# Two products of batch 1 move from VectorE to TensorE, by transposed blocks, in a fused decode-layer gradient kernel

## The chip, the core and the metric

The kernel runs on one core of a Trainium2 chip. The metric is the time of one execution on the device in microseconds; every time below is one of the core's own or comes from the hardware profile of one execution. The engines are named as in the profile: PE is TensorE's matrix products, PEld its weight loads, DVE is VectorE, ACT is ScalarE, POOL is GpSimd, SP is the engine that issues most loads.

## What is computed

The reference is one decoder layer for one new token per sequence, two sequences (batch 0 and batch 1), with its output and the gradients of seven of its inputs:

```python
h  = x + attention(layernorm(x), k_cache, v_cache, wq) @ wo   # 32 heads of 128, 4096 cached keys
h2 = h + relu(layernorm(h) @ w1) @ w2                         # 640 -> 1728 -> 640
out, vjp = jax.vjp(f, x, k_cache, v_cache, wq, wo, w1, w2)
return out, *vjp(grad_out)
```

x has 640 numbers per sequence. The caches and their gradients are the bulk: K and V hold 64 pairs of (batch, head) of 4096 x 128 bf16, one MB each, and so do their gradients. Two steps of the backward pass matter here, once per batch:

- the gradient at the input of the MLP, `w1 x gradient`: for each of the 640 rows of w1, the sum over 1728 columns of w1 times the gradient of the hidden layer (`ghfc`);
- the gradient at the attention's output, `wo x gh1`: for each of the 32 x 128 rows of wo, the sum over 640 columns of wo times `gh1`, the gradient of h.

Both sums run along the free dimension of the weights as they lie in memory (a row of the weight on a partition), which is why they are awkward for TensorE: it sums over partitions.

## The kernel before

**Two phases over 64 pairs.** The first phase (`p1_iter`, index i) reads K and V of a pair, makes the scores, the softmax and the attention output. The second (`p2_iter`, index j) reads V again (called W), makes the gradient of the probabilities by transposing W in blocks (`pair_transpose`, L436, copied out of PSUM by ScalarE at L441, multiplied at L449), and then writes two MB per pair: `gV` and `gK`, each made by VectorE in two halves (L822) and stored by GpSimd's queue (L879 and L860). An order written out by hand (`plan`) interleaves the two phases: from i = 41 on, one turn j for every two i, and after the last i the turns j alone. The second phase takes the pairs in the order of `turns`; batch 1 begins at j = 32 with its last five heads.

**A middle per batch.** `middle_gen(b)` stands between the phases of a batch: output projection, layer norm, the hidden layer (L748), for batch 1 the same again for both batches in another order (L759), then `ghfc`, then the product with w1, a layer norm backward (`ln_bwd`, whose column sum is a small product, L222), giving `gh1c`, then the products with wo. Each wo group (up to eight heads, `go_group`) yields `goc`, `gom` and `negdot`, which the turns of those heads need.

For both products the gradient is spread over all partitions (`bcast_cols`, into `fbc` and `hbc`), and VectorE multiplies and sums along the free dimension in one instruction (`ttr`, L649): 15 of 576 columns for w1 and 32 of 640 for wo, for each batch.

**Background queues.** The middle, the outer products of the weights' gradients (`fin_gen`, which makes tiles `ot` in `outer_rows`, L926, L935, L933, L937) and the gradient at x (`gx_gen`) are Python generators. Each step of a turn lets each of three queues go on by a credit: the middle by 0.8 a step up to turn 32 and 0.45 later, `fin_gen` by 0.65, `gx_gen` by 0.45. A generator says with `yield 0.9` what a piece costs. A `ttr` also waits for a slot (`turn()`): three slots a turn up to turn 32, two later. `wait(n)` lets 2n steps go by in this part. `fin_gen` begins once the w1 product is through (`("w1", 1)`), `gx_gen` goes to work once all of batch 1's wo products are.

**PSUM.** There are eight banks. 0 and 1 take the transposes, 2 and 3 the rows of a turn, 7 the middle's small results. Once the first phase is over and w1 is done, the outer products of `fin_gen` rotate over banks 4, 5 and 6; while `gx_gen` sums in bank 6, over 4 and 5:

```python
banks.update(sps=[2, 3], o=[4, 5, 6])   # when fin_gen starts
banks["o"].remove(6)                    # when gx_gen starts
```

`gx_gen` already has the form that the change gives to the two products: eight blocks of wq are transposed by TensorE (L993), copied from PSUM by ScalarE (L995), and multiplied with a column one group later (L1003).

Of the kernel before, what the change touches and what calls it, by code (L numbers as in the profile page):

```python
# [7 lines left out]
FP32 = mybir.dt.float32  # L8
# [7 lines left out]
def kernel(  # L16
# [41 lines left out]
    def f_kc(c):  # L58
        return 128 if c < NFF else F_rem
# [600 lines left out]
    def one(src, b):  # L660
        return src[:, :, b]

    def go_group(b, h0, h1, hbc):

        hs = slice(h0, h1)
        n = h1 - h0
        go32 = small.tile([128, GH], FP32, tag="go32", bufs=1, name="go32")
        for k in range(n):
            yield from turn()
            ttr(wo_t[:, h0 + k, :], hbc[:], go32[:, k:k + 1], D)  # L670
            yield 0.9
        nc.vector.tensor_copy(out=goc[:, hs, b], in_=go32[:, 0:n])
        pr = small.tile([128, GH], FP32, tag="pr", bufs=1, name="pr")
        nc.vector.tensor_tensor(out=pr[:, 0:n], in0=goc[:, hs, b], in1=OU[:, b, hs], op=ALU.mult)
        yield from wait(2)
        pair_rows(gom, goc, hs, slice(b, b + 1))
        yield from wait(2)
        d_ps = pst([128, 2, GH], FP32, "mid", "d_ps")
        nc.tensor.matmul(d_ps[:, 0, 0:n], lhsT=ones_f32, rhs=pr[:, 0:n], start=True, stop=True)
        for k in range(n):  # L680
            h = h0 + k
            nc.tensor.matmul(d_ps[:, 1, k:k + 1], lhsT=MTs.pop((b, h))[:], rhs=goc[:, h, b:b + 1],
                             start=True, stop=True)
        nc.vector.tensor_scalar(out=negdot[:, hs, b], in0=d_ps[:, 0, 0:n], scalar1=-1.0, scalar2=None, op0=ALU.mult)
        ud = small.tile([128, GH], FP32, tag="ud", bufs=1, name="ud")
        nc.vector.tensor_tensor(out=ud[:, 0:n], in0=Uc[:, b, hs], in1=negdot[:, hs, b], op=ALU.mult)
        mg = small.tile([128, GH], FP32, tag="mg", bufs=1, name="mg")
        nc.vector.tensor_tensor(out=mg[:, 0:n], in0=d_ps[:, 1, 0:n], in1=rt[:, b, hs], op=ALU.mult)
        nc.vector.tensor_tensor(out=ud[:, 0:n], in0=mg[:, 0:n], in1=ud[:, 0:n], op=ALU.add)
        nc.vector.tensor_scalar(out=GQc[:, hs, b], in0=ud[:, 0:n], scalar1=SCALE, scalar2=None, op0=ALU.mult)  # L690
        for h in range(h0, h1):
            done.add(("go", b, h))
        yield

    def mlp_out():

        ml32 = small.tile([128, ND, B], FP32, tag="ml32", bufs=1, name="ml32")
        nc.vector.memset(ml32[:], 0.0)
        for k in range(NW2):
            while free["q"] < 1:  # L700
                yield
            t = load_w2(k, "q", "(p c) d -> p c d")
            yield from wait(12)
            c1 = min(NF, (k + 1) * FP)
            m_ps = pst([128, ND, B], FP32, "mid", "mlp_ps")
            for c in range(ND):
                for cf in range(k * FP, c1):
                    kc = f_kc(cf)
                    nc.tensor.matmul(m_ps[:, c, :], lhsT=t[0:kc, cf - k * FP, c * 128:(c + 1) * 128],
                                     rhs=arow[0:kc, cf, :], start=(cf == k * FP), stop=(cf == c1 - 1))  # L710
            give(t)
            yield
            nc.vector.tensor_tensor(out=ml32[:], in0=m_ps[:], in1=ml32[:], op=ALU.add)
        ml_bf = small.tile([128, ND, B], BF16, tag="ml_bf", bufs=1, name="ml_bf")
        nc.vector.tensor_copy(out=ml_bf[:], in_=ml32[:])
        y_bf = small.tile([128, B, ND], BF16, tag="y_bf", bufs=1, name="y_bf")
        nc.vector.tensor_tensor(out=y_bf[:].rearrange("p b c -> p c b"), in0=h1c[:], in1=ml_bf[:], op=ALU.add)
        yield from wait(3)
        for b in range(B):
            store_row(y_bf[:, b, :], ND, out_0[b].rearrange("s (c p) -> (s c) p", p=128))  # L720
            yield

    def middle_gen(b):
        if o_next[0] < (b + 1) * H // OG:
# [41 lines left out]
        nc.vector.tensor_single_scalar(out=mask[:], in_=acol[:, :, b], scalar=0.0, op=ALU.is_gt)  # L766
        nc.vector.tensor_tensor(out=ghfc[:, :, b], in0=ga[:, b, :], in1=mask[:], op=ALU.mult)
        yield from wait(3)
        fbc = cols.tile([128, Dff], BF16, tag="fbc", name="fbc")
        gx2 = small.tile([128, 1, ND], FP32, tag="gx2", bufs=1, name="gx2")  # L770
        gx2p = small.tile([128, ND, 3], FP32, tag="gx2p", bufs=1, name="gx2p")
        FW = Dff // 3
        spread_f = bcast_cols(one(ghfc, b), NF, f_kc, fbc)
        have = 0
        for k in range(3):
            while have < min(Dff, (k + 1) * FW):
                next(spread_f)
                have += 512
                yield
            for c in range(ND):  # L780
                yield from turn()
                ttr(w1_t[:, c, k * FW:(k + 1) * FW], fbc[:, k * FW:(k + 1) * FW], gx2p[:, c, k:k + 1], FW)
                yield 0.85
        nc.vector.reduce_sum(out=gx2[:, 0, :], in_=gx2p[:], axis=AX.X)
        yield ("w1", b)
        yield from ln_bwd(gx2[:], x2c[:, :, b:b + 1], rstd2[:, b:b + 1], gc[:, :, b:b + 1], gh1c[:, :, b:b + 1], 1)
        hbc = cols.tile([128, D], BF16, tag="rowbc", name="hbc")
        yield from bcast_cols(one(gh1c, b), ND, lambda c: 128, hbc)
        yield ("gh1", b)

        first = H - KEPT[b]
        bounds = [(first, first + 2), (first + 2, H)] if b == 0 else [(first, H)]
        bounds += [(h, min(first, h + GH)) for h in range(0, first, GH)]
        for h0, h1 in bounds:
            yield from go_group(b, h0, h1, hbc)
        if b > 0:
            yield from mlp_out()

# [166 lines left out]
    def gx_gen(fin):  # L965
        tiles = []

        def fetch():
            while len(tiles) < ND and free["q"] > 0:
                t = take("q", [128, HD], "wqs")  # L970
                nc.sync.dma_start(out=t[:], in_=wq_r[:, len(tiles), :])
                tiles.append((t, step[0]))

        while not all(("go", B - 1, h) in done for h in range(H)):
            yield 0.0
        acc = None
        for c in range(ND):
            while c >= len(tiles) or (step[0] < tiles[c][1] + 16 and not forced[0]):
                fetch()
                yield 0.0  # L980
            if acc is None:
                banks["o"].remove(6)
                acc = ps.tile([128, ND, B], FP32, tag="bank6", bufs=1, name="gx_ps")
            t = tiles[c][0]
            todo = list(range(H))
            prev = None
            for t0 in range(0, len(todo) + GT, GT):
                part = todo[t0:t0 + GT]
                nxt = None
                if part:  # L990
                    t_ps = pst([128, GT, 128], BF16, "tps", "t_ps")
                    for x, h in enumerate(part):
                        nc.tensor.transpose(t_ps[:, x, :], t[:, h * 128:(h + 1) * 128], ident_bf[:])  # L993
                    t_sb = mats.tile([128, GT, 128], BF16, tag="XT", bufs=5, name="t_sb")
                    nc.scalar.copy(out=t_sb[:, 0:len(part), :], in_=t_ps[:, 0:len(part), :])  # L995
                    nxt = (t_sb, part)
                    if t0 + GT >= len(todo):
                        give(t)
                        fetch()
                    yield 0.9  # L1000
                if prev is not None:
                    for x, h in enumerate(prev[1]):
                        nc.tensor.matmul(acc[:, c, :], lhsT=prev[0][:, x, :], rhs=GQc[:, h, :],  # L1003
                                         start=(c == 0 and h == 0), stop=(c == ND - 1 and h == H - 1))
                    yield
                prev = nxt
        gx_bf = fin.tile([128, ND, B], BF16, tag="gxb", name="gx_bf")
        gx1b = fin.tile([128, B, ND], FP32, tag="gx1b", name="gx1b")
        nc.vector.tensor_copy(out=gx1b[:].rearrange("p b c -> p c b"), in_=acc[:])
        banks["o"].append(6)  # L1010
        yield from ln_bwd(gx1b[:], x1c[:], rstd1[:], gh1c[:], gx_bf[:], B)
        for b in range(B):
            gxo = small.tile([128, ND], BF16, tag="gxo", bufs=2, name="gxo")
            nc.vector.tensor_copy(out=gxo[:], in_=gx_bf[:, :, b])
            yield from wait(2)
            store_row(gxo[:], ND, out_1[b].rearrange("s (c p) -> (s c) p", p=128))
            yield
# [107 lines left out]
    for n, (i, j) in enumerate(plan):  # L1125
# [15 lines left out]
        if i is None and ("w1", 1) in done and fin is None:  # L1141
# [1 line left out]
            fin = tc.alloc_tile_pool(name="fin", bufs=1)  # L1143
            big2 = tc.alloc_tile_pool(name="big2", bufs=1)
            more_home("f", big2)
            banks.update(sps=[2, 3], o=[4, 5, 6])
            bg2.append(("fin", fin_gen(fin)))
            bg3.append(("gx", gx_gen(fin)))
        late[0] = all(("go", B - 1, h) in done for h in range(H))
# [84 lines left out]
```

## Time and profile before

| | |
|---|---|
| time, median of 3 | 942.42 us (935.63 to 942.82) |
| profiled execution | 939.0 us, 26775 instructions |
| TensorE products, busy | 766.9 us (82%), 11482 |
| VectorE, busy | 661.9 us (70%), 1237 |
| ScalarE, busy | 551.0 us (59%), 1162 |
| GpSimd, busy | 141.0 us (15%), 249 |
| moved by DMA | 363.02 MB, mean 387 GB/s |

Busy times are sums over the whole span. For TensorE they include the modelled end of each product, so that a busy TensorE is not TensorE at its peak. The clock that is shown with it is a share of its full speed. The busy share of DMA says how long the 16 DMA engines had a packet under way; what they moved in that time stands beside it in GB/s, and the two are not the same.

The stations of batch 1, from the trace: the hidden layer is multiplied again at 511.7 to 519.0 us (L759), the 15 products with w1 run until 562.5 us, the 32 with wo from 574.9 to 704.4 us. The first `ot` is filled at 583.2 us, the last stored at 911.0; `gx_gen` transposes from 731.5 to 868.1 us. The last gK is handed to its queue at 930.4 us.

### The profile page before, as it was taken

How to read it: one execution, taken by the hardware profiler on the slowest of the kernel's cores; microseconds unless marked ns; L12 is line 12 of the kernel's file. 1: busy time of each engine (PE TensorE's matmuls, PEld its weight loads, DVE VectorE, ACT ScalarE, POOL GpSimd, SP SyncE). 2: the span in 40 equal slices, each digit the busy share in tenths (PEclk: the TensorE clock that was granted, in tenths of full speed). 3: DMA queues.
4: the chain of work that ended last, by engine and by line, in shares of the span. 5: the costliest groups of instructions: out<-in, count | busy, mean ns of one | idle time of the engine just before them, and what ended most of it. 6: DMA issues, size and time to landing. Idle time of an engine off the chain costs nothing.

```text
span 939.0 us, 26775 instructions
## 1 busy us (share of the span) xinstructions
PE 766.9 (82%) x11482; PEld 641.4 (68%) x11482; DVE 661.9 (70%) x1237; ACT 551.0 (59%) x1162; POOL 141.0 (15%) x249
## 2 busy tenths in 40 slices
PE   6999898999998888988867838676988877887883
PEld 5878787888787777877757727564766665665652
DVE  4555677766876877786768889787797455465675
ACT  4666565667775776776633626444665564565652
POOL 1222111121001101010012112111121111021111
PEclk9999999999998999998886856556555575575556
DMA  8999999997878999999989999999999999999998
GB/s 348 418 399 410 406 394 410 412 418 266 308 280 341 360 389 423 425 422 414 419 328 369 405 426 395 395 391 376 397 406 398 425 425 423 354 389 377 333 423 364
DMA packets 59478, 363.02 MB, mean 387 GB/s; under 512 B 5696, under 2 KB 15552, under 8 KB 19168
## 3 DMA queue, kind: packets, MB, share of 16 engines
q1 hardware_dynamic: 37920, 212.18, 57.6%
q0 software_dynamic: 18432, 134.23, 34.7%
q10 hardware_dynamic: 3008, 14.91, 4.0%
q8 instruction: 90, 1.47, 0.6%
q14 instruction: 28, 0.23, 0.1%
HBM read 212.16 MB, written 149.13 MB: 385 GB/s over the span
## 4 chain that ended last, share of the span: by engine, by line
PE 39%; DMA 29%; DVE 15%; ACT 10%; issue 5%; POOL 0%; SPq 0%; POOLq 0%; DVEq 0%; ACTq 0%
DMA Kt<-in_A_k_cache_dram 12%; DMA out_dram<-gV 10%; PE t_ps L436 9%; PE m_ps L470 7%; PE t_ps L415 6%; ACT t_sb L420 5%; DMA out_dram<-gK 5%; DVE gV L822 5%; PE s_ps L426 4%; PE o_ps L926 3%; DVE gK L822 3%; DVE pk L477 2%; PE u_ps L495 2%; ACT t_sb L441 2%; DVE junk L649 2%
## 5 line engine op out<-in xcount | busy, mean ns | idle before, releaser
L420 ACT COPY t_sb<-t_ps 128x1024 bf16<-128x1024 bf16 x223 | 216.7, 1012 | 46.6 <-PE t_ps L415 41.8
L441 ACT COPY t_sb<-t_ps 128x512 f32<-128x512 f32 x256 | 149.9, 588 | 159.3 <-PE t_ps L436 156.4
L436 PE MATMUL t_ps<-ident_f,Wt 128*128 128x128 f32 x848 | 195.5, 378 | 3.7 <-ACT t_sb L995 1.4
L470 PE MATMUL m_ps<-pk,Vt 128*128 128x129 bf16 x2048 | 193.3, 224 | 1.0 <-DVE pk L477 0.6
L477 DVE TENSOR_TENSOR pk<-Kt,ep 128x2048 bf16<-128x2048 bf16 x128 | 156.3, 1221 | 34.6 <-ACT ep L520 34.5
L822 DVE TENSOR_TENSOR gK<-rb,gsp 128x2048 bf16<-128x2048 bf16 x128 | 152.2, 1224 | 32.2 <-DMA out_dram<-gK 20.1
L415 PE MATMUL t_ps<-ident_bf,Kt 128*128 128x128 bf16 x2048 | 156.8, 229 | 16.7 <-DMA Kt<-in_A_k_cache_dram 16.6
L822 DVE TENSOR_TENSOR gV<-rb,pp 128x2048 bf16<-128x2048 bf16 x128 | 152.7, 1218 | 23.3 <-DMA out_dram<-gV 20.2
L436 PEld LDWEIGHTS t_ps<-ident_f,Wt 128*128 128x128 f32 x848 | 135.8, 196 | 34.2 <-issue 23.5
L470 PEld LDWEIGHTS <-Vt 128*128 128x128 bf16 x2048 | 130.0, 100 | 29.1 <-issue 29.1
L415 PEld LDWEIGHTS <-Kt 128*128 128x128 bf16 x2048 | 129.3, 102 | 19.1 <-DMA Kt<-in_A_k_cache_dram 18.7
L449 PEld LDWEIGHTS <-t_sb 128*128 128x128 bf16 x2048 | 95.8, 106 | 40.1 <-ACT t_sb L441 18.5
L426 PE MATMUL s_ps<-qc,t_sb 128*128 128x1 bf16 x2048 | 89.2, 164 | 18.1 <-ACT t_sb L420 16.6
L449 PE MATMUL dp_ps<-gom,t_sb 128*128 128x2 bf16 x2048 | 95.2, 167 | 8.9 <-ACT t_sb L441 7.8
L426 PEld LDWEIGHTS <-t_sb 128*128 128x128 bf16 x2048 | 76.0, 97 | 30.6 <-ACT t_sb L420 27.4
L879 POOL DMA_DIRECT2D out_dram<-gV x64 | 34.2, 534 | 288.9 <-DVE gV L822 228.6
L860 POOL DMA_DIRECT2D out_dram<-gK x64 | 34.0, 531 | 279.8 <-DVE gK L822 224.7
L566 POOL COPY P_bf<-ep 128x32 bf16<-128x32 bf16 x40 | 42.6, 1065 | 220.1 <-ACT ep L520 220.1
L935 ACT CAST ot<-o_ps 128x512 bf16<-128x512 f32 (+4 forms) x134 | 60.2, 478 | 23.1 <-DMA out_dram<-ot 11.9
L561 DVE TENSOR_REDUCE rmax<-s_ps 128x1 bf16<-128x32 f32 x64 | 12.3, 193 | 61.4 <-PE s_ps L426 61.3
L649 DVE CUSTOM_DVE_ANT_0 junk<-wo_t,hbc 128x640 bf16<-128x640 bf16 x64 | 52.3, 817 | 0.2
L582 ACT CAST MT<-m_ps 128x128 bf16<-128x128 f32 x64 | 17.1, 267 | 59.1 <-PE m_ps L470 59.1
(194 smaller groups left out, 812.7 us busy)
## 6 DMA issues: line engine op xcount, KB each, us to landing
Kt<-in_A_k_cache_dram SPq DMA_DIRECT2D x64, 1024.0 KB, 14.2
Vt<-in_A_v_cache_dram SPq DMA_DIRECT2D x64, 1024.0 KB, 11.5
out_dram<-gV POOLq DMA_DIRECT2D x64, 1024.0 KB, 10.9
out_dram<-gK POOLq DMA_DIRECT2D x64, 1024.0 KB, 10.3
Wt<-in_A_v_cache_dram SPq DMA_DIRECT2D x53, 1024.0 KB, 10.8
wo_t<-in_A_wo_dram SPq DMA_DIRECT2D x4, 1280.0 KB, 14.1
wqs<-in_A_wq_dram SPq DMA_DIRECT2D x5, 1024.0 KB
wq_t<-in_A_wq_dram SPq DMA_DIRECT2D x5, 960.0 KB, 16.1
```

Source lines behind the costliest of these rows:

```text
L415: nc.tensor.transpose(t_ps[:, j, :], nat[:, g * GT + j, :], ident_bf[:])
L420: nc.scalar.copy(out=t_sb[:], in_=t_ps[:])
L426: nc.tensor.matmul(dst[:, sc:sc + 1], lhsT=t_sb[:, j, :], rhs=vec, start=True, stop=True)
L436: nc.tensor.transpose(t_ps[:, j, :], natf[:, 2 * cc:2 * cc + 2, :].rearrange("p c k -> p (c k)"), ident_f[:])
L441: nc.scalar.copy(out=t_sb[:], in_=t_ps[:])
L449: nc.tensor.matmul(dst[:, sc:sc + 2], lhsT=v[:, j, :, par], rhs=vecs[:, par, :], start=(par == 0), stop=(par == 1))
L470: nc.tensor.matmul(r["m"][:, 0:129], lhsT=r["V"][:, sc, :], rhs=r["pk"][sc // HALF][:, sc % HALF, 0:129], start=(sc == 0), stop=(sc == NSC ...
L477: nc.vector.tensor_tensor(out=p["pk"][k][:, :, 0:128].rearrange("p s (a two) -> p s a two", two=2), in0=p["K"][:, sl, :].rearrange("p s (a ...
L566: (nc.gpsimd if i < P2_AT else nc.vector).tensor_copy(out=P_bf[:, bhp, :], in_=ep[:, :, 0])
L649: nc.vector.tensor_tensor_reduce(out=junk[0:kc, 0:width], in0=in0, in1=in1, scale=1.0, scalar=0.0, op0=ALU.mult, op1=ALU.add, accum_out=acc)
L822: nc.vector.tensor_tensor(out=pairs_view(dst[:, sl, :]), in0=row.rearrange("p (a two) -> p a two", two=2)[:, None, :, :].to_broadcast([128 ...
L935: nc.scalar.copy(out=ot[0:P, k, n0:n0 + nn], in_=o_ps[0:P, 0:nn])
```

## The change

For batch 1 alone, both products leave VectorE. A helper `turned` takes them as groups of up to eight blocks of 128 x 128: TensorE transposes the blocks of a group into a bank of PSUM, ScalarE copies them to `t_sb`, and one turn of the generator later TensorE multiplies them with the gradient's column, summing in bank 6. w1 has 5 x 14 blocks (the last of each 14 has 64 columns) in ten groups, wo has 32 heads of 5 blocks, a group each. The two broadcasts of batch 1 are gone, and the pieces no longer wait for VectorE's slots. Their costs are 0.8 per w1 group and 1.2 per head. What follows the wo product (`go_done`) is as before, but reads the bank. Because bank 6 now holds these sums, the outer products of `fin_gen` have banks 4 and 5 only, until `gx_gen` has given bank 6 back. The purpose is to take the load off VectorE, and to use TensorE for it.

```diff
+    def turned(groups, cost):
+        prev = None
+        for parts in (*groups, None):
+            if prev is not None:
+                for x, (_, kc, dst, vec, first, last) in enumerate(prev[1]):
+                    nc.tensor.matmul(dst, lhsT=prev[0][0:kc, x, :], rhs=vec, start=first, stop=last)
+            if parts is not None:
+                t_ps = pst([128, GT, 128], BF16, "tps", "t_ps")
+                for x, (src, kc, *_) in enumerate(parts):
+                    nc.tensor.transpose(t_ps[0:kc, x, :], src, ident_bf[:])
+                t_sb = mats.tile([128, GT, 128], BF16, tag="XT", bufs=5, name="t_sb")
+                whole = sum(kc == 128 for _, kc, *_ in parts)
+                nc.scalar.copy(out=t_sb[:, 0:whole, :], in_=t_ps[:, 0:whole, :])
...
+            yield cost
+
+    def go_turned(b, h0, h1):
+        acc = ps.tile([128, GH], FP32, tag="bank6", bufs=1, name="go_ps")
+        yield from turned([[(wo_t[:, h, c * 128:(c + 1) * 128], 128, acc[:, h - h0:h - h0 + 1],
+                             gh1c[:, c, b:b + 1], c == 0, c == ND - 1) for c in range(ND)]
+                           for h in range(h0, h1)], 1.2)
+        yield from go_done(b, h0, h1, acc)
+
+    def gx2_turned(b, gx2):
+        acc = ps.tile([128, ND], FP32, tag="bank6", bufs=1, name="gx2_ps")
+        yield from turned([[(w1_t[:, c, cf * 128:cf * 128 + f_kc(cf)], f_kc(cf), acc[:, c:c + 1],
+                             ghfc[0:f_kc(cf), cf, b:b + 1], cf == 0, cf == NF - 1)
+                            for cf in range(f0, min(NF, f0 + GT))]
+                           for c in range(ND) for f0 in range(0, NF, GT)], 0.8)
+        nc.vector.tensor_copy(out=gx2, in_=acc[:])
...
+        if b == B - 1:
+            yield from gx2_turned(b, gx2[:, 0, :])
+        else:
+            yield from gx2_rows(b, gx2)
...
-        hbc = cols.tile([128, D], BF16, tag="rowbc", name="hbc")
-        yield from bcast_cols(one(gh1c, b), ND, lambda c: 128, hbc)
+        if b < B - 1:
+            hbc = cols.tile([128, D], BF16, tag="rowbc", name="hbc")
+            yield from bcast_cols(one(gh1c, b), ND, lambda c: 128, hbc)
...
-            yield from go_group(b, h0, h1, hbc)
+            yield from (go_group(b, h0, h1, hbc) if b < B - 1 else go_turned(b, h0, h1))
...
-                banks["o"].remove(6)
...
-            banks.update(sps=[2, 3], o=[4, 5, 6])
+            banks.update(sps=[2, 3], o=[4, 5])
```

`gx2_rows` holds the lines that stood in `middle_gen` for the w1 product, unchanged, for batch 0.

More of the change, by code (lines that the diff above doesn't have):

```diff
@@ L663, in go_group @@
     def go_group(b, h0, h1, hbc):
-        hs = slice(h0, h1)
-        n = h1 - h0
         go32 = small.tile([128, GH], FP32, tag="go32", bufs=1, name="go32")
-        for k in range(n):
+        for k in range(h1 - h0):
             yield from turn()
@@ L671, in go_group, with go_done @@
             yield 0.9
+        yield from go_done(b, h0, h1, go32)
+    def go_done(b, h0, h1, go32):
+        hs = slice(h0, h1)
+        n = h1 - h0
         nc.vector.tensor_copy(out=goc[:, hs, b], in_=go32[:, 0:n])
@@ L693, in go_group @@
         yield
+    def turned(groups, cost):
[11 more added lines that the diff above has]
+                nc.scalar.copy(out=t_sb[:, 0:whole, :], in_=t_ps[:, 0:whole, :])
+                for x, (_, kc, *_) in enumerate(parts):
+                    if kc < 128:
+                        nc.scalar.copy(out=t_sb[0:kc, x, :], in_=t_ps[0:kc, x, :])
+                prev = (t_sb, parts)
+            yield cost
[12 more added lines that the diff above has]
+        nc.vector.tensor_copy(out=gx2, in_=acc[:])
     def mlp_out():
@@ L721, in mlp_out, with gx2_rows @@
             yield
+    def gx2_rows(b, gx2):
+        fbc = cols.tile([128, Dff], BF16, tag="fbc", name="fbc")
+        gx2p = small.tile([128, ND, 3], FP32, tag="gx2p", bufs=1, name="gx2p")
+        FW = Dff // 3
+        spread_f = bcast_cols(one(ghfc, b), NF, f_kc, fbc)
+        have = 0
+        for k in range(3):
+            while have < min(Dff, (k + 1) * FW):
+                next(spread_f)
+                have += 512
+                yield
+            for c in range(ND):
+                yield from turn()
+                ttr(w1_t[:, c, k * FW:(k + 1) * FW], fbc[:, k * FW:(k + 1) * FW], gx2p[:, c, k:k + 1], FW)
+                yield 0.85
+        nc.vector.reduce_sum(out=gx2[:, 0, :], in_=gx2p[:], axis=AX.X)
     def middle_gen(b):
@@ L768, in middle_gen @@
         yield from wait(3)
-        fbc = cols.tile([128, Dff], BF16, tag="fbc", name="fbc")
         gx2 = small.tile([128, 1, ND], FP32, tag="gx2", bufs=1, name="gx2")
[L771 to L784, printed above, removed]
+        if b == B - 1:
+            yield from gx2_turned(b, gx2[:, 0, :])
+        else:
+            yield from gx2_rows(b, gx2)
         yield ("w1", b)
         yield from ln_bwd(gx2[:], x2c[:, :, b:b + 1], rstd2[:, b:b + 1], gc[:, :, b:b + 1], gh1c[:, :, b:b + 1], 1)
-        hbc = cols.tile([128, D], BF16, tag="rowbc", name="hbc")
-        yield from bcast_cols(one(gh1c, b), ND, lambda c: 128, hbc)
+        if b < B - 1:
+            hbc = cols.tile([128, D], BF16, tag="rowbc", name="hbc")
+            yield from bcast_cols(one(gh1c, b), ND, lambda c: 128, hbc)
         yield ("gh1", b)
```

## The prediction, made before the changed kernel was built

> **What bounds the kernel now.** I read the 40 slices first. In the second half the clock row of TensorE falls to 5 and 6, while the DMA row stays at 9:
>
> ```profile
> PE   6999898999998888988867838676988877887883
> DVE  4555677766876877786768889787797455465675
> ...
> PEclk9999999999998999998886856556555575575556
> DMA  8999999997878999999989999999999999999998
> ```
>
> The change lies where batch 1's products stand, from 525 us (broadcast of `ghfc`) to about 705 us (last L649). Busy time by stretch (PE, weight loads, DVE, ACT, POOL, clock, DMA share, GB/s):
>
> ```profile
> 525.00:566.00 41.00, 21.61 (x286) 17.85 (x283) 35.44 (x59) 16.37 (x31) 6.46 (x15) 0.72 1.01 415
> 566.00:702.00 136.00, 104.41 (x979) 83.16 (x979) 114.53 (x199) 74.47 (x165) 24.68 (x52) 0.56 0.99 393
> 723.00:800.00 77.00, 61.90 (x613) 45.22 (x612) 41.85 (x51) 41.70 (x88) 9.91 (x23) 0.57 1.01 425
> 800.00:880.00 80.00, 64.90 (x631) 49.65 (x630) 42.31 (x57) 47.18 (x90) 10.10 (x21) 0.56 0.94 361
> ```
>
> From 525 to 702 us VectorE is busy 150 of 177 us, and the waits of the same stretch explain nearly all the rest:
>
> ```profile
> DVE gK L822 <- DMA out_dram<-gK: 15.2, 10, 4.0
> PE csum L222 <- DVE lb_mm L290: 13.0, 1, 13.0
> ...
> PE o_ps L926 <- ACT ot L935: 13.0, 6, 5.8
> ACT ot L935 <- DMA out_dram<-ot: 11.9, 2, 6.4
> ...
> PE pr_ps L336 <- DVE goc L672: 8.8, 3, 4.0
> DVE gV L822 <- DMA out_dram<-gV: 8.1, 8, 2.5
> ```
>
> VectorE plus its 23.3 us of waiting for stores to leave a gK or gV buffer fill the stretch: VectorE and DMA share the bound. The DMA engines are always occupied, but at 398 GB/s on average against 425 later, so there is 7% in them. TensorE is busy 126 us (21.61 + 104.41) and idle 51. Its idle time is waiting for others: 13 us at the column sum L222, 9 at `pr_ps`, 13 behind ACT copies into `ot`, 12 of them a store that ACT waited for. That is the room into which the change puts work, and the whole question is whether it is enough.
>
> The later rows are what this stage may turn into. From 723 us `gx_gen` does what the change does, transposing blocks of wq, copying by ACT and multiplying one group behind, with banks 4 and 5 alone for `o_ps`. There VectorE waits 26.4 us for `dp_ps` in 157 us, TensorE paces the turns, and DMA falls to 361 GB/s in the second half.
>
> [...]L993 takes 311 ns (median), and 740 to 765 us, full of transposes, stands at clock 0.50 although TensorE is 60 to 100% busy. [...]the clock falls from 0.84 in 540 to 545 us to 0.50 as the stall of 550 to 564 us begins, and is still 0.50 fifteen microseconds after it. [...]the best 5 us stretch here shows 431[...].
>
> **VectorE, removed.** 15 products of w1 at 0.752 us = 11.3 us, 32 of wo at 0.818 us = 26.2 us: 37.5 us. `go_done`'s small operations stay. VectorE falls from 150 to about 113 us and is no bound any more.
>
> **TensorE, added.** w1: 5 x 14 blocks = 70, wo: 32 x 5 = 160; 230 transposes and 230 one-column products. L993 does 8 transposes in 1.03 us and 16 in 1.89, about 0.125 us each: 28.8 us. Products with one or two columns (L1003, L449) load 8 sets of weights in 0.29 us at best and 0.52 at worst; the middle, 0.045, gives 10.4 us. Less about 2 us of broadcasts: **+37 us**. [...]
>
> **ScalarE, added.** A copy of 1024 elements takes 1.012 us, of 512 0.588, so 640 about 0.69. w1: 5 x 1.01 + 5 x 0.69 + 5 x 0.27 for the 64-row block = 9.9 us; wo: 32 x 0.69 = 22.2 us. Less 3 us of broadcast copies: **+29 us**, 91 to 120 of 177. Not a bound by its sum, but in each group TensorE and ScalarE have to take turns.
>
> **The bank.** `o_ps` has three banks before and two after (bank 6 holds the accumulator). In `outer_rows` product x then waits for copy x-2, which stands just ahead of it, behind the copy of the last turned group on ScalarE. Behind the waiting product stand the next turn's transposes of W, and behind those `gsp`, gK and the store. Lower bound: as now with three banks, 1.8 us without the store's share for 56 products (0.03 each), so nothing. Upper bound: as from 723 to 880 us, 26.6 us for 78 products, 0.34 each: 56 x 0.31 = 17 us. I take 11, since `outer_rows` rests between tiles.
>
> **Order in time.** A turn j of the second phase has 7 background steps, each with 0.8 credit up to turn 32. Before, w1 has 3 slots a turn, 5 turns for 15 products; after, 10 groups and an empty one at 0.8 need 11 steps, 1.6 turns. A group of 8 wo products took 2.7 turns and 1.3 of waits; now 9 x 1.2 / 0.8 = 13.5 steps and 10 of waits, 3.4 turns. So `fin_gen` starts 3 to 4 turns earlier (before: 568 us) and `gx_gen` about 4 (before: 731 us). This alone gains little, as the kernel ends with turns, not with these: the last `ot` store is issued at 911 us, the last gK at 930. Four turns move from this stage's 8.0 us to the end's bare 6.4 us (7 turns from 883 to 928 us): **-6 us**.
>
> **The sum.** TensorE in the stage: 126 + 37 = 163 us; waits that stay: 12 for the store behind `ot`, 4 of the 9 at `pr_ps`, 4 at `rw_ps`, 3 of the 13 at L222, as VectorE is no longer behind; 11 for the bank: 197 us where it had 177. +20 - 6 = +14, with the earlier start of the w2 loads worth about 1: **955 us**. TensorE takes VectorE's place as the bound, because it works at half clock and is stopped by ScalarE in every group.
>
> **Rivals.** (1) *TensorE has room.* With no 13 us stall at L222 the clock stays up: TensorE's sum falls by some 15% (four transposes and their eight products of a turn take 1.15 us per group at half clock, 1.0 at full[...]), to about 139 + 25 = 164 us, under DMA. The stage then goes at DMA's 425 GB/s: 41 us x 415 + 136 x 393 = 70.5 MB, 166 us in place of 177, -11, and no more at the end: **931 us**. For it: 525 to 540 and 585 to 590 us run at clock 1.00 with just the turns' work. Against it: the `gx` stage, the same mix, stays at 0.50. (2) *A draw*: TensorE's waits absorb the added work and DMA keeps its rate of now, whatever VectorE does: **941 us**. For it: DMA share is 0.99 to 1.01 in the stage. (3) *The full price*: TensorE at half clock, the bank at 17 us, the waits at `pr_ps` and L222 stay whole: 163 + 12 + 9 + 4 + 13 + 17 = 218, +41 less 6: 977 us; I count its nearer half with the forecast.
>
> **How the numbers follow.** Forecast with its expensive tail 0.42, room and DMA gain 0.35, draw 0.23. The range goes from a little below the second (its late stage may also gain, 926) to 973, leaving out the rest of the full price. A gain of over 1% needs below 933 us, so it is nearly the room case alone.
>
> **What would show it.** Right: from 525 to 690 us the clock near 0.5 to 0.6, DMA below 390 GB/s, VectorE waiting for `dp_ps` in place of DMA, `o_ps` waiting for ACT by over 10 us more, turns at over 8.5 us; the last wo product some 30 us earlier in turns, less so in time. Wrong: clock above 0.75 there, or `o_ps` not waiting, or the turns at under 8 us with DMA near 420 GB/s; then it is the first rival. That L222 still waits 13 us would say that VectorE was behind for another reason than its products.

## The result

The changed kernel takes 972.94 us (median of 4 runs, 967.87 to 978.38) against 940.43 us for the kernel before, run beside it: ratio 1.0353, 95% interval 1.028 to 1.0426. It is slower by 32 us, where 13 were forecast. The profile below is of the execution of 978.38 us, the slowest of the four.

The 40 slices of the changed kernel, the rows that were shown of the kernel before:

```profile
PE   6999889999988888887877787777887787898982
DVE  4556667866967877778675573455676546465856
PEclk9999999999999989899855665575556555575565
DMA  9999999997788999999799696798899999999998
```

The DMA row has lost its nines just where batch 1's products stand, and VectorE's row has fallen there from digits of 7 to 9 to digits of 3 to 7 (slices 22 to 30). TensorE's row is hardly higher than it was. An engine was relieved, none became full, and the transfers ran dry. The same stretches as before (PE, weight loads, DVE, ACT, POOL, clock, DMA share, GB/s):

```profile
525.00:566.00 41.00, 32.07 (x394) 27.37 (x393) 23.04 (x32) 24.11 (x43) 6.18 (x12) 0.62 0.76 289
566.00:702.00 136.00, 105.08 (x1055) 83.14 (x1053) 70.51 (x120) 74.86 (x156) 17.23 (x39) 0.56 0.85 330
723.00:800.00 77.00, 60.87 (x572) 47.01 (x570) 46.88 (x53) 40.32 (x89) 11.91 (x27) 0.54 1.00 400
800.00:880.00 80.00, 68.56 (x725) 54.70 (x726) 46.36 (x57) 49.08 (x100) 10.68 (x25) 0.59 0.99 392
```

From 525 to 702 us DMA moved 415 and 393 GB/s before, 289 and 330 now. As the work shifts in time, the turns j are the better ruler: the time between the stores of gV, which each turn issues once. Turn 17 begins at 525 us before and at 529 us now.

| turns | before, us | after, us |
|---|---|---|
| 17 to 20 (w1 product of the changed kernel) | 24.1 | 34.1 |
| 17 to 23 | 47.8 | 56.9 |
| 23 to 36 (most of the wo products) | 109.7 | 136.2 |
| 36 to 63 (the rest, with `gx_gen`) | 245.4 | 242.9 |

The loss is 9 us at w1 and 27 at wo, and the later turns give 2.5 back. Turns 17 to 20 and 17 to 36 in the same view, first the kernel before:

```profile
524.93:545.60 20.67, 16.81 (x246) 13.71 (x244) 18.69 (x31) 13.74 (x27) 3.92 (x9) 0.95 1.01 403
524.93:682.40 157.47, 110.18 (x1124) 89.36 (x1122) 130.80 (x224) 79.39 (x172) 26.24 (x57) 0.61 1.00 397
```

and the changed kernel:

```profile
529.34:563.10 33.76, 26.40 (x326) 22.55 (x327) 16.32 (x26) 19.28 (x36) 4.40 (x9) 0.63 0.71 260
529.34:722.48 193.14, 150.45 (x1548) 120.27 (x1549) 104.41 (x163) 106.33 (x214) 26.47 (x57) 0.57 0.84 325
```

(The first line of the kernel before ends 3.4 us short of turn 20, that of the changed kernel 0.4 us.) TensorE is busy 40 us more and idle 43 us of 193, where it was idle 47 of 157: it took the new work but lost hardly any of its waiting. Who waits for whom in these turns of the changed kernel (total in us, times, longest):

```profile
DVE gsp L884 <- PE dp_ps L449: 64.0, 15, 12.0
...
ACT t_sb L712 <- PE t_ps L709: 30.5, 32, 1.5
PE o_ps L975 <- ACT ot L984: 21.3, 23, 1.3
...
PE gx_ps L705 <- ACT t_sb L712: 6.3, 6, 1.2
```

VectorE hardly waits for stores any more (6.4 us in these turns, where it waited 23); it waits for `dp_ps`, that is for TensorE, up to 12 us at a time. TensorE waits for ScalarE, 23 times for an `ot` copy, and ScalarE waits for TensorE, 32 times. What this looks like within a burst of wo heads is in order of time:

```profile
592.58 0.69 PE L709 MATMUL t_ps<-ident_bf,wo_t 128*128 128x128 bf16 x5
...
593.37 0.69 ACT L712 COPY t_sb<-t_ps 128x640 bf16<-128x640 bf16 x1 [1.19 <-PE t_ps L709]
593.96 0.58 ACT L984 CAST ot<-o_ps 96x512 bf16<-96x512 f32 x1
594.59 0.58 PE L975 MATMUL o_ps<-gr,ar 2*96 2x512 bf16 x1 [1.32 <-ACT ot L984]
595.11 0.30 PE L705 MATMUL go_ps<-gh1c,t_sb 128*128 128x1 bf16 x5
...
595.26 0.69 PE L709 MATMUL t_ps<-ident_bf,wo_t 128*128 128x128 bf16 x5
```

One head takes 2.68 us from transposes to transposes, of which TensorE waits 1.32. ScalarE copies the head's blocks, then the older `ot`; only then is one of the two banks free for `o_ps`, and behind `o_ps` on TensorE stands everything else, the next head and the next turn's transposes of W. At w1, where no `o_ps` exists yet, the products themselves wait for the copy of the group just before them (`gx_ps` in the list above).

### The profile page after: what moved, and what is told of

It is laid out like the page before. It is cut to its first block, busy times and chain, and to the rows that moved or that the text cites. A ratio compares the mean times of both kernels' runs of the same rounds, so it can differ in the third digit from the quotient of the medians.

```text
span 976.6 us, 27642 instructions
## 1 busy us (share of the span) xinstructions
PE 807.2 (83%) x11923; PEld 676.2 (69%) x11923; DVE 629.9 (64%) x1146; ACT 576.1 (59%) x1200; POOL 141.6 (14%) x249
## 4 chain that ended last, share of the span: by engine, by line
PE 45%; DMA 23%; ACT 13%; DVE 12%; issue 5%; POOL 0%; ACTq 0%; SPq 0%; POOLq 0%; DVEq 0%
DMA Kt<-in_A_k_cache_dram 15%; PE t_ps L436 13%; PE m_ps L470 6%; PE t_ps L415 5%; PE o_ps L975 5%; DMA out_dram<-gV 4%; ACT t_sb L420 4%; DMA out_dram<-gK 4%; DVE gV L871 3%; PE s_ps L426 3%; ACT t_sb L441 3%; DVE pk L477 3%; PE dp_ps L449 3%; ACT ot L984 2%; PE t_ps L709 2%
## 5 line engine op out<-in xcount | busy, mean ns | idle before, releaser
L436 PE MATMUL t_ps<-ident_f,Wt 128*128 128x128 f32 x848 | 200.9, 387 | 4.4 <-ACT t_sb L420 1.8
L436 PEld LDWEIGHTS t_ps<-ident_f,Wt 128*128 128x128 f32 x848 | 139.2, 200 | 38.4 <-issue 24.5
L871 DVE TENSOR_TENSOR gK<-rb,gsp 128x2048 bf16<-128x2048 bf16 x128 | 152.3, 1224 | 19.9 <-DMA out_dram<-gV 9.9
L884 DVE SCALAR_TENSOR_TENSOR gsp<-dp_ps,negdot,P_bf 128x64 bf16<-128x64 f32 x64 | 18.0, 281 | 93.2 <-PE dp_ps L449 92.1
L561 DVE TENSOR_REDUCE rmax<-s_ps 128x1 bf16<-128x32 f32 x64 | 12.3, 192 | 62.6 <-PE s_ps L426 62.6
## 6 DMA issues: line engine op xcount, KB each, us to landing
Vt<-in_A_v_cache_dram SPq DMA_DIRECT2D x64, 1024.0 KB, 13.1
out_dram<-gV POOLq DMA_DIRECT2D x64, 1024.0 KB, 10.2
```

The lines of the kernel that those rows point to most:

```text
L436: nc.tensor.transpose(t_ps[:, j, :], natf[:, 2 * cc:2 * cc + 2, :].rearrange("p c k -> p (c k)"), ident_f[:])
L871: nc.vector.tensor_tensor(out=pairs_view(dst[:, sl, :]), in0=row.rearrange("p (a two) -> p a two", two=2)[:, None, :, :].to_broadcast([128 ...
```

## The experiments

Each kernel was run beside the kernel before. Three theories stood at the start. *Chain*: TensorE and ScalarE stop each other in each group. *Load*: TensorE's added work at half clock (0.57 in turns 17 to 36 of the changed kernel) does not fit. *Bunching*: too many groups fall into one turn, and DMA runs dry. The first is a sharper form of the forecast's waits, the second is the body of its sum. Below, "turns 17 to 20" are turns j of the second phase; "one turn behind" and "two turns behind" count steps of the generator in `turned`.

| kernel | median us | ratio to before (95%) | turns 17 to 23 | 23 to 36 | 36 to 63 |
|---|---|---|---|---|---|
| changed kernel | 972.94 | 1.0353 (1.028 to 1.0426) | 56.9 | 136.2 | 242.9 |
| w1 alone (x_w1_only) | 944.29 | 1.0046 (1.002 to 1.0071) | 59.5 | 108.5 | 239.7 |
| wo alone (x_wo_only) | 961.11 | 1.0225 (1.0182 to 1.0268) | 49.2 | 121.2 | 254.4 |
| wo product left out (x_no_wo) | 954.15 | 1.0138 (1.0075 to 1.02) | 58.3 | 118.0 | 246.1 |
| copies left out (x_no_copy) | 945.34 | 1.006 (1.0033 to 1.0087) | 48.8 | 119.9 | 245.4 |
| kernel before, two banks (x_two_banks) | 946.26 | 1.0074 (1.0047 to 1.0101) | 47.7 | 107.0 | 251.5 |
| three banks (x_three_banks) | 958.12 | 1.0196 (1.016 to 1.0233) | 60.1 | 117.9 | 242.9 |
| copies on VectorE (x_dvecopy) | 964.53 | 1.0275 (1.0251 to 1.0299) | 57.7 | 124.1 | 241.4 |
| spread (x_spread) | 949.32 | 1.0102 (1.007 to 1.0133) | 45.6 | 111.9 | 250.7 |
| two turns behind (x_two_behind) | 957.18 | 1.0173 (1.0139 to 1.0208) | 50.2 | 128.3 | 242.1 |
| two behind, three banks (x_two_three) | 938.0 | 0.9997 (0.9975 to 1.0019) | 47.7 | 110.5 | 245.6 |
| spread, three banks (x_spread3) | 941.06 | 1.0009 (0.9985 to 1.0033) | 45.0 | 106.5 | 247.7 |
| less spread, three banks (x_spread3b) | 936.53 | 0.9969 (0.9949 to 0.9989) | 48.0 | 111.4 | 241.8 |
| half of the heads (x_half) | 942.21 | 1.0027 (1.0005 to 1.0048) | 45.8 | 114.3 | 245.1 |
| all three cures (x_all_three) | 936.07 | 0.9948 (0.9925 to 0.9972) | 44.0 | 109.2 | 244.8 |

The names in brackets are those that the expectations use. The turns are those of one profiled execution per kernel, which can lie some us from the median: 978.38 us for the changed kernel, 958.45 for the wo product left out, 949.74 for the copies left out, 940.42 for the kernel before with two banks, 943.07 for two behind with three banks. Four kernels with the same w1 burst (changed, w1 alone, wo left out, three banks) take 56.9 to 60.1 us for turns 17 to 23, so differences of 3 us and less say little. Percentages below are ratios to the kernel before, so that the runs of different hours can be compared.

**The two products apart.** Two kernels, with the lines in which each differs from the changed one (the comments are added here):

```diff
-        if b == B - 1:
-            yield from gx2_turned(b, gx2[:, 0, :])
-        else:
-            yield from gx2_rows(b, gx2)
+        yield from gx2_rows(b, gx2)                      # wo alone
...
-            yield from (go_group(b, h0, h1, hbc) if b < B - 1 else go_turned(b, h0, h1))
+            yield from go_group(b, h0, h1, hbc)          # w1 alone, with hbc spread and o=[4, 5, 6]
```

> Only the w1 product of batch 1 goes to TensorE; wo stays on VectorE, and fin_gen has its three banks. Three theories of where +32 us came from. Chain (TensorE and ScalarE stop each other in every group, made worse by the two o_ps banks): w1 runs while no o_ps exists, so it keeps its own ping-pong only, +10 us less the earlier start: 945 us. Load (37 us more TensorE work at half clock): w1 is 12 of 39 us, so a third of the loss: 950 us. Bunching (the groups come in a burst that stretches one turn and starves DMA): +10 us from the one burst of ten groups: 948 us. By the two traces turns 17 to 20 took 24 us before and 34 after.

> Only the wo products of batch 1 go to TensorE; w1 stays on VectorE. Two banks for o_ps as in the changed kernel. Chain: nearly all of the loss, as o_ps runs along: 966 us. Load: 27 of 39 us of work, two thirds of the loss: 962 us. Bunching: the four bursts of wo groups, +26 us by the two traces (turns 23 to 36: 110 us before, 136 after): 965 us. With x_w1_only it says how the loss is shared; if the two losses add up to 32 us, the parts do not help each other.

w1 loses 0.5%, wo 2.3%; together they would be 2.7%, and the change loses 3.5%. The w1 kernel meets the number of *chain* (945), the wo kernel that of *load* (962), so the pair decides nothing. w1's burst costs its 11 us (35.4 us for turns 17 to 20), but with wo on VectorE some 7 of the 12 us that turns 17 to 23 lose come back later: 1 in turns 23 to 36 with DMA at 407 GB/s, 6 in turns 36 to 63.

**The wo product left out.** `go_turned` yields as often, but uses a constant.

```diff
-        acc = ps.tile([128, GH], FP32, tag="bank6", bufs=1, name="go_ps")
-        yield from turned([[(wo_t[:, h, c * 128:(c + 1) * 128], 128, acc[:, h - h0:h - h0 + 1],
-                             gh1c[:, c, b:b + 1], c == 0, c == ND - 1) for c in range(ND)]
-                           for h in range(h0, h1)], 1.2)
+        acc = small.tile([128, GH], FP32, tag="go32", bufs=1, name="go32")
+        nc.vector.memset(acc[:], 0.01)
+        for _ in range(h0, h1 + 1):
+            yield 1.2
```

> As the changed kernel, but the wo product of batch 1 is left out (a constant takes its place, in the same steps), so neither VectorE nor TensorE does it. What is left of the loss is w1's and the earlier order. All theories: the 26 us of turns 23 to 36 go, and VectorE has 26 us less than in the kernel before. If DMA then bounds the stage at its full 425 GB/s, turns 23 to 36 take about 100 us and the whole 938 us; if DMA stays at 395 GB/s whatever VectorE does, 110 us and 948 us.

All theories missed. (The expectation's 425 GB/s is the mean of 723 to 800 us in the kernel before; that it is a ceiling was not shown.) Without any wo product the kernel is still 1.4% slower than before (0.75 to 2%), and turns 23 to 36 take 118 us at 380 GB/s, more than with VectorE doing the work. So a free VectorE brings nothing in this kernel, and something else in these turns costs some 8 us in the profiled execution, the slowest of four: `o_ps` waits 21 us for `ot` in them, on two banks; 8.7 of that is one piece, in which `ot` itself waits for a store.

**The copies left out.** TensorE does all its new work, but multiplies with the block as it lies.

```diff
-                    nc.tensor.matmul(dst, lhsT=prev[0][0:kc, x, :], rhs=vec, start=first, stop=last)
+                    nc.tensor.matmul(dst, lhsT=prev[1][x][0][0:kc, 0:128] if kc == 128 else w1_t[0:kc, 0, 0:128], rhs=vec, start=first, stop=last)
...
-                t_sb = mats.tile([128, GT, 128], BF16, tag="XT", bufs=5, name="t_sb")
-                whole = sum(kc == 128 for _, kc, *_ in parts)
-                nc.scalar.copy(out=t_sb[:, 0:whole, :], in_=t_ps[:, 0:whole, :])
...
-                prev = (t_sb, parts)
+                prev = (None, parts)
```

> As the changed kernel, but ScalarE's copies of the turned blocks are left out: TensorE transposes as before and multiplies with the block as it lies, so TensorE's work is the same, and nothing waits for a copy. Chain: most of the loss goes, as neither the products nor o_ps wait for a copy of a group: 950 us, o_ps waiting for ACT under 8 us from 529 us on (25 in the changed kernel). Load: next to nothing changes: 968 us. Bunching: the bursts get shorter by the waits but stay, 955 us.

0.6% in place of 3.5%: 230 transposes and 230 products stay, and five sixths of the loss are gone. This fells *load* as far as it means that the added work does not fit. But TensorE's busy time fell as well, in turns 17 to 36 from 150.5 to 134.8 us, with the clock at 0.66 in place of 0.57; what the work costs at a low clock cannot be read from this run. w1's turns 17 to 20 take 24.0 us, as before the change, with its whole work on TensorE.

**The bank.** First in the kernel before, by itself:

```diff
-            banks.update(sps=[2, 3], o=[4, 5, 6])
+            banks.update(sps=[2, 3], o=[4, 5])
...
-                banks["o"].remove(6)
```

> The kernel before, with only the bank taken: o_ps rotates over banks 4 and 5 from the start of fin_gen, both products stay on VectorE. If the bank costs something by itself (the kernel without the wo product took 118 us for turns 23 to 36, where the one with three banks and VectorE's wo product took 108): turns 23 to 36 about 118 us, 950 us in all. If the bank only matters together with the turned groups: 941 us, no change.

It costs 0.7% without any turned group, by the median of eleven executions. Where it costs that is not shown: the profiled execution is the fastest of the eleven, hardly slower than the kernel before, and in it turns 23 to 36 do not lose (107.0 us) while 36 to 63 lose 6 us. Then the other way, the changed kernel with three banks for `o_ps` until `gx_gen` starts; `go_turned` has its own loop, otherwise as `turned`:

```diff
+                g_ps = pst([128, 1], FP32, "mid", "go_ps")
+                for c in range(ND):
+                    nc.tensor.matmul(g_ps[:], lhsT=prev[0][:, c, :], rhs=gh1c[:, c, b:b + 1],
+                                     start=(c == 0), stop=(c == ND - 1))
+                nc.scalar.copy(out=acc[:, prev[1] - h0:prev[1] - h0 + 1], in_=g_ps[:])
...
+            banks.update(sps=[2, 3], o=[4, 5, 6])
```

> The changed kernel with o_ps on banks 4, 5 and 6: a wo head's sums go to the small results' bank 7, and ScalarE copies each column out at once. Chain with the bank: o_ps no longer waits for a copy that stands behind a head's copy; its wait for ACT falls from 21 to under 8 us in turns 23 to 36, which go from 136 to 120 us: 957 us. If the copies cost by themselves (products waiting for their copy[...]): 130 us, 967 us.

As the chain said: turns 23 to 36 fall from 136.2 to 117.9 us, and 1.6% of the 3.5 are back. `o_ps` waits for ScalarE under 3 us in these turns, where it was 21.0. Turns 23 to 36 of the changed kernel and of this one:

```profile
586.25:722.48 136.23, 105.68 (x1021) 83.01 (x1021) 71.73 (x112) 72.54 (x148) 17.68 (x39) 0.54 0.85 324
582.41:700.27 117.86, 106.92 (x1034) 84.46 (x1033) 72.15 (x113) 75.15 (x173) 18.98 (x39) 0.53 0.95 369
```

TensorE is busy as long as without the cure and at the same clock, 0.54 and 0.53; its idle time falls from 31 to 11 us. Here the loss is the standing still.

**Another engine for the copies.** `nc.scalar.copy` in `turned` becomes `nc.vector.tensor_copy`.

> The changed kernel with the copies of the turned blocks on VectorE, which is idle for almost half of that stage, and the rest as it is. Chain through ScalarE (the ot copy stands behind the head's copy on ScalarE): o_ps waits for ACT under 10 us, turns 23 to 36 take 120 us: 957 us. If what costs is that TensorE waits for any copy one turn behind, or if the copies come late because VectorE waits for stores: no gain, 970 us or more.

Between the two: 0.8% back. `o_ps` waits 11.3 us in place of 21.0 in turns 23 to 36, but VectorE now waits 15.3 us there for the transposes, and TensorE at w1 for VectorE (3.1 us at the products in turns 17 to 20).

**Fewer groups in a turn.**

```diff
-                           for h in range(h0, h1)], 1.2)
+                           for h in range(h0, h1)], 2.4)
...
-                           for c in range(ND) for f0 in range(0, NF, GT)], 0.8)
+                           for c in range(ND) for f0 in range(0, NF, GT)], 2.4)
```

> The changed kernel with the groups spread: a w1 group costs 2.4 of credit in place of 0.8, a head 2.4 in place of 1.2, so that fewer fall into one turn. Bunching: the same work lies beside more turns, DMA does not run dry: 952 us. Chain: each group costs its waits wherever it stands, only the order changes: 968 us.

2.5% back, the most of any single cure, with two banks and every copy in place. Turns 17 to 36 take 157.5 us, exactly the kernel before. What is left stands in turns 36 to 63, 5 us more than before: part of the work now lies there, with the last wo product at 789 us, in turn 48 (685 us and turn 31 in the changed kernel), and `gx_gen` begins at 828 us. By this run alone, bunching would be the cause. But the kernel without copies kept the bursts and lost still less, so the loss needs both.

**One turn more between copy and product.**

```diff
-        prev = None
-        for parts in (*groups, None):
-            if prev is not None:
-                for x, (_, kc, dst, vec, first, last) in enumerate(prev[1]):
-                    nc.tensor.matmul(dst, lhsT=prev[0][0:kc, x, :], rhs=vec, start=first, stop=last)
+        made = []
+        for n, parts in enumerate((*groups, None, None)):
+            if n > 1:
+                t_sb, old = made.pop(0)
+                for x, (_, kc, dst, vec, first, last) in enumerate(old):
+                    nc.tensor.matmul(dst, lhsT=t_sb[0:kc, x, :], rhs=vec, start=first, stop=last)
...
-                prev = (t_sb, parts)
+                made.append((t_sb, parts))
```

> The changed kernel with its bursts and two banks, but each group's products two turns of the generator behind their copy in place of one. If TensorE's waiting for the copy of the group just before is the loss: turns 17 to 23 fall from 57 to 49 us, 23 to 36 from 136 to 125: 955 us. If what counts is the burst and o_ps standing behind the copy: 23 to 36 stay at 134, 968 us.

1.8% back. The ten w1 groups cost nothing any more, burst or not. Turns 17 to 20 and 17 to 36 of this kernel, to be held beside the 33.76 and 193.14 us of the changed one (same columns):

```profile
524.12:548.29 24.17, 21.04 (x350) 17.96 (x350) 16.55 (x26) 20.88 (x40) 3.91 (x9) 1.00 0.98 365
524.12:702.59 178.47, 132.83 (x1542) 105.48 (x1541) 103.72 (x163) 105.02 (x214) 28.74 (x57) 0.68 0.92 354
```

The same w1 work 10 us sooner, and the clock at 1.00 where it was 0.63. From the first transpose of the w1 burst to its last product it is 14.2 us in place of 22.9, half by shorter waiting (TensorE idle 1.9 us, not 6.4) and half by faster work (busy 12.3 us, not 16.5, at a clock of 0.98 in place of 0.57). The second line says the same of the whole stretch: TensorE is idle 46 us, no less than in the changed kernel (43); what fell is its busy time, by 18 us, at 0.68 in place of 0.57. So *load* is not quite out: the work of these turns kept TensorE busy for 150.5 us at 0.57 and for 132.8 us at 0.68. Whether the clock was low because of the waits is not shown, as no run changed the clock by itself. At wo, 128.3 us remain in turns 23 to 36, for `o_ps` still waits 19.9 us.

**Both waits cut, the bursts kept.** This was the run that had to decide whether a burst costs by itself: two turns behind, three banks, credits as in the change.

> The changed kernel with its bursts (0.8 and 1.2), but with both waits of a burst cut: products two turns behind their copy, and three banks for o_ps. If the bursts cost only through these two waits: turns 17 to 23 as with two turns behind (50 us), 23 to 36 at 112 us, 941 us. If a burst costs by itself, because its work is too much for the one turn it falls into: 118 us as with three banks alone, 948 us.

938.0 us, no difference from the kernel before. Turns 17 to 20 and 17 to 36 of this kernel:

```profile
526.46:550.09 23.63, 21.40 (x292) 18.99 (x293) 16.36 (x25) 17.49 (x34) 3.93 (x10) 0.78 0.99 368
526.46:684.68 158.22, 141.18 (x1558) 115.20 (x1558) 104.34 (x165) 109.19 (x250) 28.59 (x57) 0.63 1.00 398
```

and of its waits in these turns

```profile
DVE gsp L899 <- PE dp_ps L449: 40.1, 13, 5.8
ACT t_sb L441 <- PE t_ps L436: 27.7, 50, 2.6
...
ACT t_sb L737 <- PE t_ps L735: 6.3, 20, 0.9
...
DVE gV L886 <- DMA out_dram<-gV: 5.3, 4, 2.5
```

All the work of the change, all of its bursts, in 158 us as in the kernel before (157.5), although this execution is 5 us above its kernel's median. VectorE still waits 40 us for TensorE, in pieces of under 6 us, and DMA moves 398 GB/s as before the change (397). The 0.78 of the first line is a mean: to 537.5 us, where the w1 burst ends but for its last products, this kernel too stands at 1.00, and at 0.59 after it. Turns 17 to 36 side by side:

| kernel | us | TensorE busy | idle | clock |
|---|---|---|---|---|
| before | 157.5 | 110.2 | 47.3 | 0.61 |
| changed | 193.1 | 150.5 | 42.7 | 0.57 |
| three banks | 178.0 | 155.5 | 22.5 | 0.54 |
| two turns behind | 178.5 | 132.8 | 45.6 | 0.68 |
| both | 158.2 | 141.2 | 17.0 | 0.63 |

The third bank takes away idle time; the second turn takes away busy time above all. The single cures were worth 1.6 and 1.8%, together 3.6: within the intervals they add up, and with them the loss is complete.

**Is there a gain in it?** Four kernels on three banks, with a costlier credit, a smaller change, or all cures at once:

> Both cures: groups spread (2.4 per w1 group and per head) and three banks for o_ps. Bunching and bank are separate losses (23 us and 7 to 15 us by the single cures): 934 to 940 us, at least as fast as the kernel before, with 'o_ps waits for ACT' under 8 us in turns 17 to 36. If they are one loss, cured already by spreading, this stays at 947 us.

> As x_spread3 with less spreading (w1 group 1.6, head 1.8), so that the wo products are through sooner and gx_gen starts sooner. If the late start of gx_gen is what is left of the loss: faster than x_spread3, 933 us. If bunching counts in proportion: between the two, 943 us.

> w1 on TensorE, spread; of the wo heads every second stays on VectorE (in its slots), the others go to TensorE, with three banks. Neither engine gets the whole load: if the stage is then held by DMA alone, turns 17 to 36 take 152 us in place of 157 and the whole is 933 us. If the stage was held by DMA before anyway: 940 us.

In this last one (x_half), the even heads of a group take VectorE's way:

```diff
+            if h is not None and (h - h0) % 2 == 0:
+                yield from turn()
+                ttr(wo_t[:, h, :], hbc[:], acc[:, h - h0:h - h0 + 1], D)
+                yield 0.9
+                continue
```

> All three cures: two turns behind, three banks, spread to 1.6 and 1.8. If the waits and the burst are separate: faster than x_spread3b (936.5 us), 932 us. If spreading already covers what the second turn behind would: the same, 936 us.

Spread to 2.4 with three banks the kernel equals the one before, a little short of what was expected. With 1.6 and 1.8 it is 0.3% faster (0.11 to 0.51%), with the second turn behind 0.5% (0.28 to 0.75%), the best of all; these two intervals overlap, so it is not shown that the second turn adds anything once the groups are spread. Sharing the heads between the engines gains nothing: turns 17 to 36 take 160 us, not 152. In the best kernel they take 153 us, 4 less than before, at DMA share 1.01 and 399 to 411 GB/s. More was not found in a free VectorE.

**Open.** Without the wo product turns 23 to 36 took 118 us. It is not that more products of `fin_gen` fall into them, though it starts two turns earlier: 45 `o_ps` products are recorded there, 44 in the kernel before. The reason was not found. Nor is it shown in which turns the bank costs its 0.7% in the kernel before, or what raises and lowers the clock.

## Why the prediction was wrong

The side was right, the size was not, and the step that failed is the sum of waits that stay: 34 us, without the products' wait for the copy one turn before them. Put on turns 17 to 36, where TensorE was busy 110 us before, the forecast gives 110 + 37 + 34 = 181 us; 193 were measured, 150.5 busy and 42.7 idle. What stood in the place of the 34 was a wait of `o_ps` behind the copies on two banks (15 us by its cure, 11 forecast) and the products' wait for their copy (17 us by its cure, nothing forecast). The later turns gave back 2.5 us and not 6.

- *VectorE, removed, and no bound any more.* Right: busy 150 us from 525 to 702 us before, 109 from 529 to 728 us after, and few waits for stores. L222 no longer waits in the changed kernel, where it waited 13 us, nor with w1 alone on TensorE, but it does with wo alone there (13.1 us): VectorE had been behind because of its w1 products.
- *TensorE, added, +37 us.* The size is right (busy +40 in turns 17 to 36), at the clock that the changed kernel had. But the forecast took the low clock as given by the kind of work. With both waits cut the same work makes +31 us at 0.63, and the 47 us that TensorE stood idle before take it in at no cost. The 13 us at the column sum and the 9 at `pr_ps` were an engine ahead of VectorE, and went when it had other work; the store behind `ot` was not waited for any more either.
- *ScalarE, added, +29 us.* Right (+27), and "take turns" named the place. It was not priced.
- *The bank, 11 us, from 0 to 17.* Too small by a little: 1.6% or 15 us by the run with three banks.
- *The term that was missing.* The products' wait for the copy one turn before them was not in the sum at all; `gx_gen`, the row from which it was read, has other work between its groups (0.45 of credit a step against 0.8), and its products (L1003) wait for no copy. By the run two turns behind it is 1.8%, 17 us, which includes the slower work at the lower clock.
- *Luck in the sum.* Of the 34 us, 19 did not stay: the 12 for the store, the 4 at `pr_ps` and the 3 at L222. In their place came 21 us at `o_ps` and 10 at the products of the groups (`gx_ps`, `go_ps`). That the sum still comes within 9 us of the idle time is luck.
- *Order in time, -6 us.* Turns 36 to 63 give 2.5 us back.
- *The signs named beforehand*: clock 0.57, DMA 325 GB/s, VectorE waiting for `dp_ps`, turns of 10.2 us, the last wo product in turn 31 in place of 39, at 685 us in place of 704. These came; `o_ps` waited 21.3 us for ScalarE in turns 17 to 36 against 13.0, a little less than the 10 more that were named. The size was wrong all the same: signs of a wait do not tell its size or its cause.
- *The rivals.* The second, the draw at 941 us, is what the kernel is once it does not wait: 938.0 us, with DMA at its rate of before, 398 GB/s. The first, that TensorE has room and the stage goes at the 425 GB/s of 723 to 800 us, did not come: even the best kernel, 936.07 us, has 399 to 411 GB/s and a clock of 0.64 in turns 17 to 36. Nor did the clock stay up without the stall at L222: neither the changed kernel nor w1 alone has that stall, and they stand at 0.64 and 0.59 in turns 17 to 23, at 0.54 and 0.56 in turns 23 to 36.

The forecast held TensorE to half of its full clock, as 740 to 765 us of the kernel before, with transposes of wq and W, stood at 0.50; that the transposes were the reason is not shown by any run. The line of turns 17 to 20 with two turns behind has 1.00 with 58 recorded transposes of w1 and 21 of wo added to the turns' own. So the clock was full in a stretch in which more than half of the time of TensorE's products was that of transposes (16 of 28 us, added up). What raised it was not tried by itself. The kernel before had said so already: its `gx_gen` stage does not stay at 0.50, as the first rival's text has it, but stands at 0.97 and 1.00 from 765 to 775 us, with the transposes of L993 among its work: 32 of them lie from 766 to 776 us, with a median of 219 ns where that of all 160 is 311. And the fall of the clock that was read together with the stall at L222 came first: from 545 to 550 us it stood at 0.50 with TensorE busy half of the time, and the stall began at 551.

## What to carry to other kernels

Before pricing work that is moved to an idle engine, ask what the engine will stand still for on its way. With an order fixed in the program, a step TensorE to ScalarE to TensorE that was one turn deep had nothing to hide its round trip in the bursts of this kernel (10.4 us of waits of the groups' products for their copies in turns 17 to 36), though TensorE was idle for 43 of the 193 us there. Two turns of distance and one more bank made 230 transposes and as many products free here, where the same work with one turn and two banks cost 3.5%. When both leaving out the copies and spreading the groups cure a loss, neither is the whole cause: keep the one, cut the other, and see. And after a cure, look whether idle time or busy time fell: in turns 17 to 36 the third bank took 20 us from TensorE's idle time (42.7 to 22.5), the second turn 18 us from its busy time (150.5 to 132.8).

## What was not expected of the hardware

In the bursts of the ten w1 groups the clock went with the gaps rather than with the kind of work. With six waits of the products for their copy, 6.3 us in all, a transpose of w1 took 314 ns (median) in the changed kernel and in the one with three banks, and the burst stood at 0.57 and 0.50. With 1.0 us of such waits or less it took 219 ns: 0.98 and 0.97 in the two kernels with two turns behind, 1.00 in the one without copies. It is no rule: the spread kernel has 0.50 to 0.52 to 536 us and 1.00 from there on, in the midst of its w1 groups, and the third bank took half of TensorE's idle time out of turns 17 to 36 without raising the clock (0.57 and 0.54).

And freeing VectorE hardly let DMA move more. In turns 23 to 36 VectorE was busy 89 of 110 us in the kernel before and 71 of 111 with both waits cut; DMA moved 392 and 398 GB/s, at a share of 1.00 and 1.01. TensorE was busy 99 of the 111 us, so it may be what holds the turns there; that was not tried.
